# A scheduler that reckons with the arrival of TensorE's instructions: a linear-attention and hardswish kernel, its order set anew

## The chip, the cores and the metric

The kernel runs on one core of a Trainium2 chip. The metric is the device time of one execution in microseconds (us), the median of several runs. The profile is that of one execution.

Engines are named as in the profile: PE is TensorE (PEld its weight loads), DVE is VectorE, ACT is ScalarE, POOL is GpSimd, and SP is SyncE, which issues almost all transfers. SBUF tiles and PSUM banks are named as in the code.

## The reference

Two parts, one behind the other. The first is a linear attention with a decaying state, for 4 batches, 8 heads, 768 steps and a head size of 48:

```python
for t in range(S):
    cur = np.einsum('bhd,bhe->bhde', u[None] * kt, vt)
    y[:, :, t] = np.einsum('bhd,bhde->bhe', rt, state + cur)
    state = wt[:, :, :, None] * state + np.einsum('bhd,bhe->bhde', kt, vt)
```

The second takes its output as 3072 tokens of 384 and applies two matrices (384 to 2048 and back) with a hardswish between them:

```python
h = x @ w_in
g = h * np.clip(h + 3.0, 0.0, 6.0) / 6.0
return (g @ w_out).astype(np.float32)
```

## The kernel before

The sequence is cut into 24 chunks of 128 steps, and four chunks make one of six blocks of 512 tokens. For each chunk `i` the kernel has a set of small steps, whose names in the program's plan are used in this document:

- `feat{i}` and `tok{i}` load the chunk (SP, L394 and L406). `back{i}` and `fore{i}` are scans over the decays on DVE (L469, L478); `K{i}` (L489) and `R{i}` (L493) scale keys and queries by them; `own{i}` (L502) and, on PE, `dot{i}` (L516) give the step's own term; `diag0{i}` and `diag1{i}` (L534, ACT) put it on a diagonal, four instructions each.
- `score{i}` (L544, PE) multiplies K and R into two PSUM banks; `above{i}` (L551) takes the masked result from there.
- `turn{i}` (L560, PE) transposes K, `turned{i}` (L565, ACT) copies it out, `kv{i}` (L646, PE) multiplies it with the values, and `kvs{i}` (L654, ACT) copies the product out of its banks; `decay`, `mid`, `decb`, `state` carry the state on.
- `read{i}` (L624 and L633, PE) gives the chunk's output and `leave{i}` (L711, L713 or L729, ACT) copies it out as the second part's input. For chunks 0 and 1 the last pair of heads goes ahead: `first{i}` on PE, `third{i}` (L693, L695, ACT), and then `read{i}`, which here begins with L703.

The weights arrive as 64-bit words in sixteen portions of two slices (`fetch{j}`, L437, 768 KB each, into a ring of three tiles named `bits`). Each is made into float32 by one step on ACT, `low{j}` (L447, output `more`), and two on DVE, `whole{j}` (L451) and `full{j}` (L456).

The second part of block 0 is done directly: `up0.{f}.{c0}` (L762, PE), `ramp` (L752, ACT), `gate` (L773, DVE), `down0.{c}.{q}` (L781, PE). Blocks 1 to 5 use fast matrix products with fewer multiplications: `tx` (sums of inputs, DVE), `up{bk}.{d}.{r}` (L876, PE), `read`, `clip` and `gate` of these (L884 to L901, ACT and DVE), `sum` (L916, DVE), `down` (L931, PE) and `out` (L940 to L949).

None of this stands in the code in the order in which it runs. All steps are handed to a class `Plan`, each with its engine, a duration, the steps it comes after, the ring slots that it takes and what frees them, and a key (a due time). `order()` goes through them like a simulation: on each engine the step that can start at the earliest time is taken, and among those ready the one with the least key. Transfers are reckoned with one shared link (`link`, `RATE`, `LAND`). `SHIFT` is a table of single numbers, each added to one step's key. `emit()` then issues the instructions in that order. As every engine runs its own instructions in the order of issue, this fixes the order on every engine. Where `emit` finds PE idle by the plan's times, before the first `up`, it issues filler matmuls (`spin`, L1315, into a bank that nobody reads):

```python
k = int((self.start[n] - last + self.MORE) / self.SPIN) if n != self.until else 0
while k > 0:
    self.spin(min(k, 4))
    k -= 4
```

Of the kernel before, what the change touches and what calls it, by code (L numbers as in the profile page):

```python
# [24 lines left out]
BC = 4  # L25
# [5 lines left out]
TURN = 1.0  # L31
# [18 lines left out]
    "feat0": -208.0, "tok0": -511.0, "own0": 640.0, "feat1": -504.0, "feat2": -267.0, "tok2": 624.0, "own2": 100.0,  # L50
    "score2": -447.0, "decay2": -430.0, "read2": -592.0, "fore3": 878.0, "R3": 1602.0, "turn3": 238.0, "fore4":
    1394.0, "dot4": 93.0, "above4": -46.0, "turn4": 171.0, "dot5": 251.0, "diag05": 1476.0, "kv5": 701.0, "decay5":
    916.0, "back6": 349.0, "fore6": 289.0, "tok7": -372.0, "tok8": -269.0, "read8": 595.0, "leave8": 181.0, "tok9":
    -130.0, "mid9": 1100.0, "leave9": 780.0, "tok10": -62.0, "fore10": 1238.0, "kvs10": -128.0, "fore11": 364.0,
    "back12": -176.0, "kvs12": -271.0, "kvs13": -325.0, "leave13": 519.0, "feat14": -376.0, "feat15": -211.0,
    "back15": 735.0, "fore15": 867.0, "own15": 553.0, "diag015": 343.0, "turn15": -96.0, "fore16": -151.0, "sum16":
    -625.0, "turn16": 381.0, "kvs16": -750.0, "state16": 575.0, "fore17": 567.0, "back18": 607.0, "diag018": 281.0,
    "fore19": 793.0, "ownu19": 638.0, "diag019": 77.0, "back20": 445.0, "sum20": 541.0, "feat22": -92.0, "fetch1":
    71.0, "fetch2": -265.0, "fetch3": 477.0, "fetch5": 558.0, "whole5": 411.0, "full7": 831.0, "fetch8": 617.0,
    "fetch9": 453.0, "full9": 571.0, "fetch10": 474.0, "whole10": 464.0, "fetch11": 1041.0, "fetch12": 1125.0,  # L60
    "fetch13": 605.0, "fetch14": 909.0, "fetch15": 1157.0, "up0.4.0": 612.0, "up0.5.0": 782.0, "up0.6.0": 410.0,
    "gate0.6.0": 250.0, "up0.7.0": 510.0, "gate0.7.0": 82.0, "up0.12.0": 225.0, "up0.13.2": 490.0, "down0.0.1":
    436.0, "down0.2.0": 173.0, "tx1.4": 929.0, "up1.0.14": 105.0, "up1.0.8": 106.0, "up1.0.16": 112.0, "up1.1.14":
    190.0, "up1.1.0": 759.0, "up1.1.8": 421.0, "up1.1.17": -327.0, "up1.1.1": 185.0, "up1.1.9": 237.0, "up1.1.2":
    253.0, "down1.0.1.0": 1079.0, "down1.0.3.0": 113.0, "down1.0.7.0": 111.0, "sum1.1.4.0": -503.0, "sum1.1.1.1":
    -483.0, "sum1.1.3.1": 446.0, "sum1.1.4.1": -357.0, "down1.1.1.0": 819.0, "down1.1.5.0": 630.0, "down1.1.2.1":
    536.0, "down1.1.3.1": 901.0, "down1.1.7.0": -52.0, "down1.1.7.1": -163.0, "down1.1.4.1": -398.0, "up2.0.14":
    -59.0, "up2.0.6": 277.0, "up2.0.0": 389.0, "up2.0.8": -182.0, "up2.0.15": -137.0, "up2.0.12": -138.0,
    "up2.0.17": -172.0, "up2.0.1": -455.0, "up2.0.9": -77.0, "up2.0.13": -144.0, "up2.0.2": 229.0, "read2.0.a13":
    -521.0, "gate2.0.1": -124.0, "gate2.0.5": 68.0, "gate2.0.6": -53.0, "up2.1.14": -107.0, "up2.1.8": 236.4,  # L70
    "up2.1.11": 912.0, "up2.1.18": 331.0, "up2.1.9": 250.0, "read2.1.a7": -96.0, "down2.0.6.0": -9.0, "down2.0.6.1":
    -122.0, "down2.0.3.0": -22.0, "down2.0.3.1": -136.0, "down2.0.7.1": 101.0, "down2.1.1.0": -497.0, "down2.1.5.0":
    540.0, "down2.1.2.1": 524.0, "down2.1.7.0": -938.0, "down2.1.7.1": -482.0, "down2.1.4.1": 291.0, "tx3.1":
    -946.0, "tx3.6": -620.0, "tx3.7": -728.0, "tx3.9": -953.0, "tx3.10": -697.0, "up3.0.5": 367.0, "up3.0.12":
    392.0, "up3.0.17": 365.0, "up3.0.7": 341.0, "read3.0.a3": 599.0, "read3.0.a11": 519.0, "gate3.0.0": 423.0,
    "gate3.0.2": 673.0, "clip3.0.3": 753.0, "clip3.0.7": 825.0, "up3.1.6": 342.0, "up3.1.8": 398.0, "up3.1.12":
    730.0, "up3.1.11": 266.0, "up3.1.1": 376.0, "up3.1.18": 278.0, "up3.1.13": 395.0, "clip3.1.5": 693.0,
    "down3.0.6.0": -301.0, "down3.1.5.0": 184.0, "up4.0.14": -773.0, "up4.1.14": -82.0, "up4.1.12": -53.0,
    "up4.1.1": -129.0, "down4.0.1.0": 465.0, "down4.0.5.1": 668.0, "down4.1.1.0": -128.0, "down4.1.3.1": 311.0,
    "up5.0.12": 268.0, "up5.0.3": 180.0, "up5.0.9": 47.0, "up5.1.19": 256.0, "up5.1.6": 260.0, "up5.1.0": -418.0,  # L80
    "up5.1.8": 324.0, "up5.1.12": -67.0, "up5.1.1": 132.0, "up5.1.3": 260.0, "up5.1.9": 236.0, "read5.1.a9": 1037.0,
    "down5.0.1.0": 407.0, "down5.0.4.1": 534.0, "refetch0": -312.0, "refetch1": -670.0, "refetch2": -706.0,
    "refetch3": -338.0, "refetch4": -348.0, "refetch5": 538.0, "refetch8": -563.0, "refetch9": -330.0, "vet9.1":
    424.0, "refetch15": -227.0, "vet15.1": -951.0, "vet17.0": 413.0, "refetch18": -176.0
# [73 lines left out]
class Plan:  # L158
# [14 lines left out]

    def lag(self, a, n):

        engine = self.steps[a][0]
        if engine != self.steps[n][0]:
            return self.HOP[engine]
        kind = a.split(".")[0].rstrip("0123456789")
        alike = kind == n.split(".")[0].rstrip("0123456789")  # L180
        return self.CHAIN if engine == "DVE" and not (alike and kind in self.LONE) else None

    def __init__(self):
        self.steps = {}
        self.rings = {}
        self.taken = {}
# [4 lines left out]
    def add(self, name, engine, us, emit, after=(), key=0.0, hold=(), port=False, kb=0.0, lands=0.0,  # L191
            dmas=1):

        assert name not in self.steps, name
        self.steps[name] = (engine, us, emit, tuple(after), key + SHIFT.get(name, 0.0), tuple(hold), port, kb, lands, dmas)

# [6 lines left out]
    def order(self):  # L203
# [5 lines left out]
        lanes = []  # L209
        left = {n: sum(a not in end for a in x[3]) for n, x in steps.items()}  # L210
# [7 lines left out]
        while open_:  # L218
# [30 lines left out]
            free[engine] = end[n] = t + us  # L249
# [25 lines left out]
    def emit(self):  # L275

        last = self.COLD
        spinning = self.spin is not None
        for n in self.order():
            engine, us, emit = self.steps[n][:3]  # L280
            if engine == "PE" and spinning:
                k = int((self.start[n] - last + self.MORE) / self.SPIN) if n != self.until else 0
                while k > 0:
                    self.spin(min(k, 4))
                    k -= 4
                last = self.start[n] + us
                spinning = n != self.until
            emit()


def fast_path(tc, feat, tok, wflat, ub, ug, moe_w_in, moe_w_out, out, flag, n_chunks):
# [21 lines left out]
    with ExitStack() as ctx:  # L313
# [696 lines left out]
        def do(fn, *args):  # L1010
            return lambda: fn(*args)
# [27 lines left out]
        for i in range(NT):  # L1039
# [21 lines left out]
            if i < BY_PE:  # L1061
                plan.add(f"own{i}", "DVE", 0.56, do(own, i), [f"feat{i}"] + ["later"] * (i == 0) + [f"own{i - 1}"] * (i > 0), k + OWN,
                         [("rk", [f"dot{i}"])], port=True)
                plan.add(f"dot{i}", "PE", 0.82, do(own_dot, i), [f"own{i}"], k + OWN, [("ps", [f"sum{i}"])])
# [10 lines left out]
            if i <= BC:  # L1075
                plan.add(f"score{i}", "PE", 0.55, do(score, i), [f"K{i}", f"R{i}"] + [f"score{i - 1}"] * (i > 0), due,
                         [("bank", [f"above{i}"])] * 2)
            plan.add(f"above{i}", "DVE", 0.68, do(above, i), [scored(i), f"diag1{i}"], due + 0.5)
            plan.add(f"turn{i}", "PE", 0.39 if i <= BC + 1 else 0.44, do(turn_k, i), [f"K{i}"] + [f"turn{i - 1}"] * (i > 0), due + 0.01 if i <= BC + 1 else due - TURN, [("ps", [f"turned{i}"])])
            plan.add(f"turned{i}", "ACT", 0.42, do(turned_k, i), [f"turn{i}"] + [f"turned{i - 1}"] * (i > 0), due - 2 if i > BC + 1 else due + 0.5,  # L1080
                     [("kn", [written_by(i)])])
            if i in SOLO:
                plan.add(f"kv{i}", "PE", 0.5, do(write_alone, i), [f"turned{i}", f"tok{i}"], t - 0.2,
                         [("bank", [f"kvs{i}"])] * 2)
# [18 lines left out]
            if i < BY_SUM:  # L1103
                plan.add(f"first{i}", "PE", 0.65 if first else 0.75, do(read_last, i), [f"above{i}", f"decb{i}"], t + 0.01, y)
                plan.add(f"third{i}", "ACT", 0.54 if i != APART else 0.9, do(leave_last, i), [f"first{i}"], t + 0.01,
                         ([("x", all_up), ("S_", [f"read{j}" for j in range(BY_SUM)])] if i == 0 else []))
                plan.add(f"read{i}", "PE", 2.6 if first else 2.95, do(read_rest, i), [f"third{i}"], t + 0.01)
                plan.add(f"leave{i}", "ACT", 1.05, do(leave_rest, i), [f"read{i}"], t + 0.02)
            elif bk == 0:
                plan.add(f"read{i}", "PE", 1.5, do(read_both, i), [f"above{i}", f"decb{i}"], t + 0.01, y)  # L1110
                plan.add(f"leave{i}", "ACT", 1.5, do(leave, i), [f"read{i}"], t + 0.02)
            else:
                uses = [f"up{bk}.{d}.{r}" for d in range(2) for r in range(20) if X_PLACE[r][0] == "w"] + [f"tx{bk}.{x}" for x in range(len(X_SUMS))]
                space = [("x", uses)] * (c == 0)
                needs, us, hold = [begun(i), f"above{i}"], 0.52, []
                reads = [f"above{i + 1}"]
                if i + 2 < NT and i + 2 not in SOLO:
                    needs += [f"turned{i + 2}", f"tok{i + 2}"]
                    reads += [f"kvs{i + 2}"]
                    us += 0.42  # L1120
                if i + 1 < NT:
                    needs += [f"R{i + 1}", f"K{i + 1}", f"decb{i + 1}"]
                    hold = [("bank", reads)] * 2 + [("y", [f"leave{i + 1}"])]
                    us += 1.05
                if i == BC:
                    plan.add(f"begin{i}", "PE", 0.6, do(begin, i), [f"decb{i}", f"R{i}", f"read{i - 1}"], t - LEAD, y)
                plan.add(f"read{i}", "PE", us, do(read, i), needs, t + 0.01, hold)
# [24 lines left out]
        for x, (c0, c1) in enumerate(parts):  # L1152
            m = c1 - c0
            for f in range(NFC):
# [3 lines left out]
                         k, [("bank", [f"gate{n_}"])])  # L1158
# [4 lines left out]
        for c in classic:  # L1163
            for q in range(HF):
# [4 lines left out]
                         [("bank", [f"drain0.{c}"])] if q == 0 else ())  # L1169
# [44 lines left out]
        for bk in range(NB):  # L1214
# [7 lines left out]
            for d in range(2 * (bk > 0)):  # L1222
# [19 lines left out]
                for c, items in enumerate(CHAINS):  # L1242
                    for j_, x in enumerate(items):
                        if not isinstance(x, int):
# [4 lines left out]
                                 [("bank", [r + items[-1]])] if j_ == 0 else ())  # L1249
# [17 lines left out]
            for p in range(2 * (bk > 0)):  # L1267
# [12 lines left out]
                for n_, (k_, after, hold) in enumerate((  # L1280
                        (1, [], [("bank", [r + "c21"])]), (5, [], [("bank", [r + "c12"])]), (2, [r + "s1"], []),
                        (6, [r + "s1"], []), (3, [r + "v"], []), (7, [r + "u"], []), (4, [r + "c22"], []))):
                    for x in range(2):
                        before = gated(0, NFC) if k_ != 1 else gated(4 * x, 4 * x + 4)
                        if k_ in (5, 6, 7, 3):
# [3 lines left out]
                                 before + [d_ + f"{k_}.0"] * x + [d_ + f"{chain}.1"] * bool(chain) + after + [f"sout{t_}.{x}" for t_ in ({5: 1, 6: 2, 7: 3, 4: 4}.get(k_),) if t_], at + 2.6 * n_ + 1.3 * x + (2.6 if k_ == 4 else 0), hold if x == 0 else ())  # L1289
# [368 lines left out]
```

## Time and profile before

| | |
|---|---|
| Runs | 547.68, 545.11, 547.29 us; median 547.29 |
| Profiled execution | 547.55 us; span from first to last instruction 545.8 us |
| PE busy | 532.4 us (98%), 5408 matmuls |
| DVE, ACT, POOL busy | 425.3, 255.9, 113.7 us |
| First `up` (L762) starts | 34.56 us |
| Granted PE clock, mean | 0.992 |
| Data queue (q1) | 63.12 MB, 38.4% of the 16 transfer engines' span |
| Instruction queue of PE (q8) | 44 packets, 0.72 MB |

Times within the execution are counted from the span's start. A busy time is the union of an engine's instructions; a stretch in which PE is busy is not for that reason at full pace, since fillers count as busy and the granted clock may be below 1. "A <- B" in a list of waits means that A's engine stood until B's event, by the order of the semaphores' times; that the event named was the last one near by is no proof that it was waited for.

### The profile page before, as it was taken

How to read it: one execution, taken by the hardware profiler on the slowest of the kernel's cores; microseconds unless marked ns; L12 is line 12 of the kernel's file. 1: busy time of each engine (PE TensorE's matmuls, PEld its weight loads, DVE VectorE, ACT ScalarE, POOL GpSimd, SP SyncE). 2: the span in 40 equal slices, each digit the busy share in tenths (PEclk: the TensorE clock that was granted, in tenths of full speed). 3: DMA queues.
4: the chain of work that ended last, by engine and by line, in shares of the span. 5: the costliest groups of instructions: out<-in, count | busy, mean ns of one | idle time of the engine just before them, and what ended most of it. 6: DMA issues, size and time to landing. Idle time of an engine off the chain costs nothing.

```text
span 545.8 us, 13085 instructions
## 1 busy us (share of the span) xinstructions
PE 532.4 (98%) x5408; PEld 465.8 (85%) x5408; DVE 425.3 (78%) x701; ACT 255.9 (47%) x656; POOL 113.7 (21%) x111
## 2 busy tenths in 40 slices
PE   8979999999999999999999999999999999999996
PEld 5768787666788999988999988999888999988995
DVE  6969899997768989999876989998858843188450
ACT  3857655543255844365335554744254632353300
POOL 2000010765100554413042215253200300000000
PEclk9979999999999999999999999999999999999999
DMA  8996695443110168765034773056300000000001
GB/s 222 276 247 199 173 302 177 130 115 111 57 38 1 34 196 246 232 203 160 1 97 155 272 235 81 23 188 232 125 0 1 17 25 23 30 0 1 0 16 49
DMA packets 23267, 64.03 MB, mean 117 GB/s; under 512 B 3216, under 2 KB 10544, under 8 KB 23200
## 3 DMA queue, kind: packets, MB, share of 16 engines
q1 hardware_dynamic: 23072, 63.12, 38.4%
q8 instruction: 44, 0.72, 0.5%
q14 instruction: 23, 0.19, 0.1%
q10 hardware_dynamic: 128, 0.00, 0.0%
HBM read 57.31 MB, written 4.72 MB: 114 GB/s over the span
## 4 chain that ended last, share of the span: by engine, by line
PE 89%; DMA 6%; DVE 2%; ACT 1%; issue 1%; SPq 1%; DVEq 0%; ACTq 0%
PE bank L931 28%; PE bank L876 27%; PE bank L781 8%; PE bank L762 6%; PE bankS L931 5%; PE bankS L876 5%; DMA bits<-in_moe_w_in_dram 4%; PE bank L544 2%; PE bank L646 2%; PE y_ps L633 2%; PE y_ps L624 2%; DMA bits<-in_moe_w_out_dram 2%; PE ps L560 1%; PE ps L516 1%; ACT xT L729 0%
## 5 line engine op out<-in xcount | busy, mean ns | idle before, releaser
L897 ACT ACTIVATE clip<-g,three 128x512 f32<-128x512 f32 x80 | 56.8, 721 | 56.2 <-DVE g L893 45.2
L893 DVE TENSOR_TENSOR g<-bank,g 128x512 f32<-128x512 f32 x80 | 53.8, 684 | 16.2 <-PE bank L876 11.2
L901 DVE SCALAR_TENSOR_TENSOR g<-clip,g 128x512 f32<-128x512 f32 x80 | 57.2, 731 | 6.4 <-ACT clip L897 6.1
L489 POOL TENSOR_TENSOR K<-feat_in,E 112x512 f32<-112x512 f32 x17 | 24.7, 1453 | 161.1 <-PE bank L544 133.7
L931 PE MATMUL bank<-w_out,g 128*128 128x192 f32 x320 | 56.9, 328 | 0.0
L931 PEld LDWEIGHTS bank<-w_out,g 128*128 128x128 f32 x320 | 52.6, 190 | 1.1 <-issue 0.2
L534 ACT ACTIVATE A<-eyes,dg 128x64 f32<-128x64 f32 x192 | 49.0, 336 | 1.7 <-PE y_ps L633 1.3
L762 PE MATMUL bank<-xT,w_in 128*128 128x256 f32 x192 | 44.9, 386 | 0.0
L729 ACT COPY xT<-y_ps 48x256 f32<-48x256 f32 x88 | 32.2, 366 | 24.1 <-PE y_ps L624 21.7
L781 PE MATMUL bank<-w_out,g 128*128 128x384 f32 x128 | 42.8, 489 | 0.0
L762 PEld LDWEIGHTS bank<-xT,w_in 128*128 128x128 f32 x192 | 36.0, 193 | 5.0
L876 PE MATMUL bank<-xT,w_in 128*128 128x256 f32 x160 | 40.2, 381 | 0.0
L891 ACT COPY g<-bank 128x512 f32<-128x512 f32 x50 | 28.5, 586 | 21.1 <-PE bank L876 21.0
L781 PEld LDWEIGHTS bank<-w_out,g 128*128 128x128 f32 x128 | 24.0, 190 | 15.5
L947 ACT ACTIVATE o<-bank 128x192 f32<-128x192 f32 x30 | 9.9, 330 | 57.4 <-PE bank L931 57.2
L505 POOL TENSOR_TENSOR rk<-rk_in 128x384 f32<-128x384 f32 x15 | 16.3, 1089 | 94.9 <-PE ps L516 71.9
L876 PEld LDWEIGHTS bank<-xT,w_in 128*128 128x128 f32 x160 | 29.9, 190 | 4.7 <-ACT g L891 1.1
L478 DVE TENSOR_TENSOR_SCAN W<-feat_in,start 112x520 f32<-112x520 f32 x24 | 33.4, 1395 | 0.5 <-PE y_ps L624 0.5
L469 DVE TENSOR_TENSOR_SCAN E<-feat_in,back 112x520 f32<-112x520 f32 x24 | 30.4, 1268 | 3.3 <-DMA feat_in<-in_feat_dram 3.1
L876 PE MATMUL bank<-xT,bits 128*128 128x256 f32 x120 | 30.6, 381 | 0.0
L493 POOL TENSOR_TENSOR W<-feat_in,W 112x512 f32<-112x512 f32 x17 | 24.4, 1438 | 25.1 <-DVE W L478 25.1
L931 PE MATMUL bankS<-w_out,g 128*128 128x192 f32 x160 | 28.6, 329 | 0.0
(274 smaller groups left out, 1122.4 us busy)
## 6 DMA issues: line engine op xcount, KB each, us to landing
feat_in<-in_feat_dram SPq DMA_DIRECT2D x23, 675.9 KB, 5.8
bits<-in_moe_w_in_dram SPq DMA_DIRECT2D x8, 768.0 KB, 12.9
bits<-in_moe_w_out_dram SPq DMA_DIRECT2D x8, 768.0 KB, 5.5
feat_in<-in_moe_w_in_dram SPq DMA_DIRECT2D x8, 768.0 KB, 4.7
feat_in<-in_moe_w_out_dram SPq DMA_DIRECT2D x8, 768.0 KB, 5.6
rk_in<-in_tok_dram SPq DMA_DIRECT2D x15, 384.0 KB, 5.9
v_in<-in_tok_dram SPq DMA_DIRECT2D x24, 192.0 KB, 4.6
out_dram<-o SPq DMA_DIRECT2D x24, 192.0 KB, 2.1
```

Of the source, the lines that this page charges most:

```text
L469: nc.vector.tensor_tensor_scan(out=E_[:, ::-1], data0=d["w"][:, :0:-1], data1=back.rearrange("q p t -> q (p t)")[:, ::-1], initial=0.0, op ...
L478: nc.vector.tensor_tensor_scan(out=W_, data0=d["w"][:, :-1], data1=starts[i % 2].rearrange("q p t -> q (p t)"), initial=0.0, op0=ALU.mult, ...
L534: nc.scalar.activation(out=d["A"][:, h, :], in_=eyes, func=ACT.Copy, scale=d["dg"][:, h])
L729: nc.scalar.copy(out=blocks[bk]["xT"][g * GP:g * GP + D, :, at:at + HL], in_=st[i]["y_ps"][y_bank(i, a, g)][(g ^ a) * GP:(g ^ a) * GP + D, ...
L762: nc.tensor.matmul(h_ps[:, :(c1 - c0) * L], lhsT=w_in[:, f // 2, j, f % 2, :], rhs=b["xT"][:, j, c0 * L:c1 * L], start=(j == 0), stop=(j = ...
L781: nc.tensor.matmul(b["o", c][:, :DM], lhsT=g_of(0, f, c), rhs=w_out[:, f, :], start=(f == 0), stop=(f == NFC - 1))
L876: nc.tensor.matmul(b["p", d, c][:, z * HB:(z + 1) * HB], lhsT=weight(W_PLACE[r])[:, 2 * z + d, :], rhs=x_at(bk, X_PLACE[r]), start=fresh a ...
L891: nc.scalar.copy(out=out_, in_=src)
L893: nc.vector.tensor_tensor(out=out_, in0=src, in1=out_of(bk, d, other), op=ALU.add if sign > 0 else ALU.subtract)
L897: nc.scalar.activation(out=c, in_=out_of(bk, d, u), func=ACT.Relu, bias=three, scale=1.0)
L901: nc.vector.scalar_tensor_tensor(out=g, in0=blocks[bk]["r", d, u], scalar=6.0, in1=g, op0=ALU.min, op1=ALU.mult)
L931: nc.tensor.matmul(b["d", p, to][:, :h], lhsT=a, rhs=w(), start=(f == 0 and k in (1, 5)), stop=(f == HF - 1 and k in (2, 3, 4)), skip_grou ...
```

## The change

`Plan` now keeps, for each PE step, a number of instructions (`size`), and walks a counter through PE's instruction stream. Every 256 instructions (`PORTION`) a further portion is asked for when the counter passes a mark (`ASKED`), and the portion asked for before that one has to be there when it passes a second mark (`NEEDED`). A portion arrives a fixed time after it was asked for (`FETCH`), plus a share of what the data link still has to move at that moment (`BEHIND`, at most `MOST`). Where it is late, the PE step's planned end moves by as much; fillers are reckoned as instructions too. The durations, dependencies and rings of all steps are unchanged. The table `SHIFT` is replaced as a whole, so that the order of steps differs on every engine, from the first microseconds to the last block.

```diff
 SHIFT = {
-    "feat0": -208.0, "tok0": -511.0, "own0": 640.0, "feat1": -504.0, "feat2": -267.0, "tok2": 624.0, "own2": 100.0,
...
+    "feat0": -505.0, "tok0": -422.0, "own0": 1325.0, "decb0": 271.0, "feat1": -407.0, "tok1": -297.0, "feat2":
...
 }
@@ class Plan
+    PORTION, ASKED, NEEDED = 256, 168, 194
+    FETCH, BEHIND, MOST = 3.5, 1.2, 8.0
+    before = 8
+
+    def passed(self, f, t, us, size, link):
+
+        late, i0 = 0.0, f["at"]
+        while size > 0 and self.PORTION * f["n"] + self.ASKED < i0 + size:
+            asked, needed = self.PORTION * f["n"] + self.ASKED, self.PORTION * f["n"] + self.NEEDED
+            asked = max(t + late + us * max(0.0, asked - i0) / size, f["ready"])
+            needed = t + late + us * min(1.0, max(0.0, needed - i0) / size)
+            late += max(0.0, f["ready"] - needed)
+            f["ready"] = asked + self.FETCH + min(self.MOST, self.BEHIND * max(0.0, link - asked))
+            f["n"] += 1
+        f["at"] = i0 + max(size, 0)
+        return late
+
+    def fills(self, start, last):
+
+        return max(0, int((start - last + self.MORE) / self.SPIN))
@@ order()
             start[n] = t
-            free[engine] = end[n] = t + us
+            late = 0.0
+            if engine == "PE":
+                k = self.fills(t, last) if filling and n != self.until else 0
+                filling = filling and n != self.until
+                if k:
+                    late = self.passed(fetch, t - k * 0.213, k * 0.213, 4 * -(-k // 4), link)
+                late += self.passed(fetch, t + late, us, self.size[n], link)
+                last = t + us + late
+            free[engine] = end[n] = t + us + late
@@ emit()
-                k = int((self.start[n] - last + self.MORE) / self.SPIN) if n != self.until else 0
+                k = self.fills(self.start[n], last) if n != self.until else 0
...
-                last = self.start[n] + us
+                last = self.end[n]
@@ fast_path: every step on PE gets its size, as in
-                plan.add(f"dot{i}", "PE", 0.82, do(own_dot, i), [f"own{i}"], k + OWN, [("ps", [f"sum{i}"])])
+                plan.add(f"dot{i}", "PE", 0.82, do(own_dot, i), [f"own{i}"], k + OWN, [("ps", [f"sum{i}"])], size=16.7)
...
```

## The prediction

> **What bounds the kernel now.** I read the page first (TensorE, PE, is busy nearly the whole span), then the stretches, then who waits for whom, the chain, the transfers and ScalarE's timeline where PE stands still. All times come from one profiled execution: 547.55 us, of which 545.8 are the span and 1.7 lie around it; it stands 0.26 above the median of 547.29.
>
> ```profile
> span 545.8 us, 13085 instructions
> ...
> PE 532.4 (98%) x5408; PEld 465.8 (85%) x5408; DVE 425.3 (78%) x701; ACT 255.9 (47%) x656; POOL 113.7 (21%) x111
> ...
> q8 instruction: 44, 0.72, 0.5%
> ```
>
> The work of PE is the same after the change, so only the time in which it stands, spins or runs at half clock can move. The stretches (length, then busy time of each engine, granted clock, transfer share, GB/s) show where that is:
>
> ```profile
> 16.50:28.00 11.50, 11.02 (x197) 8.74 (x194) 11.11 (x20) 8.74 (x28) 0.00 (x0) 1.00 1.05 283
> 28.00:31.50 3.50, 0.05 (x4) 0.05 (x4) 1.03 (x3) 2.06 (x5) 0.00 (x0) 0.62 1.02 221
> 31.50:36.00 4.50, 4.50 (x45) 4.09 (x46) 3.30 (x8) 1.37 (x6) 0.00 (x0) 0.54 1.05 259
> 36.00:60.00 24.00, 23.73 (x326) 20.11 (x325) 19.47 (x36) 16.66 (x44) 0.00 (x0) 1.00 0.78 220
> 60.00:66.00 6.00, 5.38 (x116) 4.24 (x115) 5.79 (x13) 4.42 (x17) 0.00 (x0) 1.00 0.27 65
> 66.00:100.00 34.00, 33.88 (x272) 27.06 (x271) 32.36 (x57) 19.30 (x43) 6.14 (x5) 1.00 0.65 217
> 100.00:322.00 222.00, 222.00 (x2463) 192.31 (x2462) 191.20 (x295) 107.86 (x291) 71.31 (x62) 1.00 0.44 135
> 322.00:541.00 219.00, 217.47 (x1850) 200.80 (x1848) 149.04 (x252) 87.88 (x201) 33.28 (x30) 1.00 0.17 54
> ```
>
> One hole is long: 28 to 31.5, followed by a stretch at a clock of 0.54. PE's own waits put it down so:
>
> ```profile
> PE bank L544 <- ACT more L447: 3.6, 1, 3.6
> PE bankS L1315 <- POOL ident masks.py:199: 1.4, 1, 1.4
> PE bank L876 <- DVE T__4259 L828: 0.7, 1, 0.7
> ```
>
> L544 is `score2`. It reads K and R of chunk 2 and never `more`; K was done at 20.66, R (L493) at 25.38, and its banks were free by 28.8 at the latest. So the releaser named is only the last event near by. What does fit is in the transfers of 28 to 30 us, one packet of PE's instruction queue (it runs from 28.47 to 29.83):
>
> ```profile
> q8 instruction: 1, 0.02, 4.2%
> ```
>
> Between 20 and 28 us that queue moved nothing, and PE had run 346 matmuls and 346 weight loads when it stopped. I take it that PE stood for its next portion. ScalarE (ACT) in the same time:
>
> ```profile
> 22.85 1.08 ACT L447 ACTIVATE more<-bits 128x768 int16<-128x768 uint8 x1 [0.23 <-DMA bits<-in_moe_w_in_dram]
> 23.80 0.61 ACT L693 COPY xT<-bank 48x64 f32<-48x64 f32 x4
> ...
> 25.30 2.02 ACT L534 ACTIVATE A<-eyes,dg 128x64 f32<-128x64 f32 x8
> 27.85 0.32 ACT L711 COPY xT<-bank 128x192 f32<-128x192 f32 x1 [0.53 <-PE bank L633]
> 28.18 0.64 ACT L713 COPY xT<-bank 64x192 f32<-64x192 f32 x2
> ...
> 30.03 1.06 ACT L447 ACTIVATE more<-bits 128x768 int16<-128x768 uint8 x1 [0.98 <-DMA bits<-in_moe_w_in_dram]
> ```
>
> Here `leave1` (L711, L713), which the first `up` product needs, is done at 28.8, ahead of the `low` step at 30.03 that waits for the fourth portion of weights. Before the change nothing but PE's stop holds the first `up`, which starts at 34.56.
>
> **The stop's price.** Idle from 27.82 to 31.45: 3.63 us. After it the same groups run slow: L544 x32 1.13 for 0.70 elsewhere, L516 x8 2.05 for 1.04, L762 x6 2.12 for 1.47, together 2.1. In all 5.7 us, 1.0% of the time: the most that this part can bring.
>
> The page Runtime: NRT & Kernel Launch of the Trainium skill, section Instruction fetch mechanics, says that PE's program memory is refilled in blocks of 16 KiB (256 instructions), ahead of their use, and that crossing a block's edge is mostly hidden. The packet sizes agree (44 packets, 0.72 MB); the 3.63 us do not look hidden. By that rule there is nothing to remove, and this part would be worth 0 in place of at most 5.7.
>
> **What the new order puts there.** I followed the changed program's instructions as they stand on each engine. The fetch reckoning itself adds no instruction; fillers (L1315) go from 15 to 13, worth nothing by themselves since they only fill waits. On SP the first twelve transfers are the same, the twelfth being the fourth portion of weights (issued at 20.14, landed at 30.01); then two more weight portions go ahead of two `feat` loads. On ACT two things move. `leave0` now stands behind two `low` steps, and `third1` behind `leave0`. And `leave1` now stands behind the `low` of that fourth portion and four more diagonals.
>
> 1. `third1` to `read1`. The third portion's `low` ends at 23.93 (row above); `leave0` 0.96 and `third1` 0.61 follow: 25.4. PE has `kv1`, `read0`, `first1`, `dot2` and one filler until about 23.0 (it issues `turn2` and `kv2` later now), so it stands some 2.4 us. `read1` then takes 2.5 (L703 1.45, L624 0.54, L633 0.55): 27.9. `dot3` and `score2` (1.04 and 0.70) bring it to 29.6.
> 2. The first `up`. Landing 30.01, `low` 1.06, four diagonals 1.0 (half of 2.02), `leave1` 0.32 and 0.64, 0.15 to PE: 33.2. PE stands again, 3.6 us. The instruction portion's packet, some 1.6 us before PE goes on at 31.45, now falls under this wait: the 692nd PE instruction is at the end of `score2`. If the portion of weights lands earlier, since no `feat` load runs beside it, the least is 26.66 (the transfer before it) plus 786 KB at the 390 GB/s that weights alone reached at 17 to 20 us, 28.7, and the first `up` 31.9. I take 33.2, by the row of the same transfer.
> 3. Work not yet done. `turn2` and `kv2` come later on PE: 0.44 and 0.61, 1.05 us. So the first `up` at 33.2 for 34.56 is a gain of 1.36 - 1.05 = 0.3 (1.6 at best).
> 4. Clock. Before, it dropped 1.0 us into the stop, for 6.8 us, 1.1 us of them after 34.56 (0.55 lost). Two holes of 2.4 and 3.6 us will do so at least once: I take 2.9 us after 33.2, 1.45 lost, so 0.9 worse; between 0.55 better (clock back by then) and 1.2 worse.
>
> So the stop is replaced by ACT's queue, not removed: 0.6 us slower up to 36 us, between 2.1 faster and 1.5 slower.
>
> **From 36 to 66 us.** Before, PE stands 0.27 and 0.62 here; the longest, 0.53 before an L516, is behind L654, behind an L447 that waited 2.30 for a portion of `w_out` landed at 57.59. In the new order `kvs3`, then `leave2`, stand right behind the `low` of SP's twenty-first transfer, and `score3` on PE needs the banks that `kvs3` frees. Need: 33.2 plus ten `up` (1.30 each), two `turn`, two `kv`, one `dot` (1.0), `read2` (1.4) and the lost clock: 52.1. Offer: transfers twelve to twenty-one are 6.5 MB; after 26.66 they take 22.9 us at 283 GB/s or 27 at 240 (rows of 16.5 and of 28 to 36), so 49.6 to 53.7, plus `low` 1.06 and `kvs3` 0.55: 51.2 to 55.3. PE waits 0 to 3.2 us. I take 1.1, near the middle, less the 0.5 that goes: 0.6 slower.
>
> **From 66 us on.** Idle time is 0.12, 0 and 1.53, so at most 1.65 to gain; the orders of the blocks are new throughout, and they can lose as much. No row prices a single move; I take 0, plus or minus 1.6. The 5 us after the last matmul stay.
>
> Sum: 547.55 + 0.6 + 0.6 - 0.26 = 548.5.
>
> **The rivals.**
> - The stop goes and little follows. For: weights were moved at 390 GB/s where no `feat` load ran beside. Against: `leave1` behind a `low`. First `up` at 31.9 with the clock back (2.1), no wait at `score3` (0.5), half of the late idle time (0.8): 3.4 less, 543.9. The bound, with all 5.7 kept, is 541.6.
> - ACT blocked, slower. Price, if the twenty-first transfer lands at 53.7: PE stands 3.2 at `score3`, and the clock falls again (2.1 as at 31.5), less 0.5, plus 0.6 from the start: 5.4 more, 552.7. It decides from a landing after about 52.5. For: ACT is strictly in order, and seven more `low` steps stand among `kvs` and `leave` steps there. Against: only 0.5 us came through before.
> - The change does not do what it says: instructions are late at the portion before (packet at 17.77). PE would stand 1 to 2 us near 20, inside the wait for `third1` anyway: 548.5 again, counted with the forecast.
>
> **How the numbers follow.** No change within measurement is 0.5% (2.7 us), about what this kernel can tell. Forecast 0.48, first rival 0.2, second 0.32. Some of the first rival's cases stay under 2.7 us and some of the forecast's upper end goes over: faster 0.17, same 0.5, slower 0.33. The range reaches 5 us both ways, to below the faster case and past the slower one, with about one in ten outside at each end; the likeliest case alone is 546 to 551.
>
> **What would show it.** Right: in the new profile PE's idle time before L584 or the first L802 of the new numbering, near 29 to 33 us, ended by ACT `xT` (leave1), and another near 23 to 25 ended by ACT `xT` (third1); the first L802 at 32 to 33.5; clock below 1 in 28 to 36. Steps 1 and 2 are wrong if PE runs through from 20 to 36. The 36 to 66 part is wrong if no wait on ACT `kvs` shows there. The whole is wrong if PE's idle time after 66 us changes by over 2 us.

## The result, and the profile after

| | before | changed |
|---|---|---|
| Median of 20 executions | 546.44 us (545.11 to 549.10) | 548.17 us (545.83 to 552.37) |
| Profiled execution, span | 547.55, 545.8 us | 546.18, 544.5 us |
| A second profiled execution of the changed kernel | | 547.81, 546.1 us |
| First `up` starts | 34.35 (34.56 if counted from the end of the matmul before it) | 29.45; in the second 30.59 |

The ratio of the changed kernel to the one before is 1.0033, interval 1.0017 to 1.0050: 0.3% slower, inside the bound of 0.5%. The profiled execution is one of the quickest of its kernel: its granted clock was 0.996, and of the twenty executions the five at 0.996 or above took 545.8 to 547.2 us, the fifteen at 0.993 or below 547.5 to 552.4. So two profiles are read here: this one, and the second (run `a_again` below) for what most executions do.

From the page of the changed kernel:

```profile
span 544.5 us, 13050 instructions
...
PE 530.7 (97%) x5404; PEld 462.7 (85%) x5404; DVE 421.7 (77%) x701; ACT 256.1 (47%) x656; POOL 112.8 (21%) x111
...
q8 instruction: 44, 0.72, 0.6%
```

The same stretches as before the change (length, busy time of PE, PEld, DVE, ACT, POOL, granted clock, transfer share, GB/s):

```profile
16.50:28.00 11.50, 9.44 (x161) 7.52 (x161) 11.25 (x19) 7.11 (x22) 0.00 (x0) 1.00 1.03 300
28.00:31.50 3.50, 2.73 (x42) 2.36 (x42) 3.40 (x7) 2.62 (x9) 0.00 (x0) 1.00 1.11 297
31.50:36.00 4.50, 4.15 (x19) 3.34 (x18) 3.50 (x8) 4.00 (x12) 0.00 (x0) 1.00 0.98 226
36.00:60.00 24.00, 23.75 (x326) 19.92 (x325) 23.80 (x49) 19.83 (x55) 0.00 (x0) 1.00 0.88 291
60.00:66.00 6.00, 6.00 (x59) 4.79 (x58) 5.99 (x12) 2.66 (x5) 0.00 (x0) 1.00 0.86 236
...
322.00:541.00 219.00, 214.46 (x1837) 198.05 (x1835) 149.44 (x249) 86.49 (x199) 30.95 (x30) 1.00 0.18 57
```

The hole of 3.5 us is gone, and 16.5 to 28 us, once nearly full, now lacks 2.1 us of PE. In the last stretch PE ends at 538.38, so 2.6 of the 4.5 us that are missing lie after the last matmul; the other 1.9 are waits. PE's own waits name them:

```profile
PE bank L743 <- ACT xT L733: 0.9, 1, 0.9
PE ps L556 <- DVE rk L542: 0.8, 1, 0.8
PE bank L802 <- ACT xT L753: 0.8, 1, 0.8
PE bank L971 <- DVE S__3772 L956: 0.6, 1, 0.6
PE bank L916 <- DVE g L933: 0.6, 1, 0.6
PE bank L916 <- ACT g L931: 0.4, 1, 0.4
```

The first three lie at 22.5, 26.1 and 28.7 us (`third1`, `own3` on DVE, `leave1`); the last three at 325 to 343 us are new, for before the change PE waits for nothing between 300 and 350. ACT's timeline at the start:

```profile
20.95 1.09 ACT L487 ACTIVATE more<-bits 128x768 int16<-128x768 uint8 x1 [1.34 <-DMA bits<-in_moe_w_in_dram]
...
22.86 0.64 ACT L733 COPY xT<-bank 48x64 f32<-48x64 f32 x4
...
26.57 1.07 ACT L487 ACTIVATE more<-bits 128x768 int16<-128x768 uint8 x1 [1.78 <-DMA bits<-in_moe_w_in_dram]
...
28.45 0.30 ACT L751 COPY xT<-bank 128x192 f32<-128x192 f32 x1
28.76 0.64 ACT L753 COPY xT<-bank 64x192 f32<-64x192 f32 x2
```

The queue is as forecast (`leave0` and `third1` behind two `low` steps, `leave1` behind the next and four diagonals), but that next `low` starts at 26.57 and not at 30.01: the fourth portion of weights landed at 26.49, 3.5 us earlier than before.

**Where PE falls behind.** A view made from the traces: at a given time, that time less the work PE has done, each matmul counted with the median pace of its kind at full clock in the profile before (510.3 us in all, for every kernel here). What a stretch adds to it is idle time, fillers, half clock and slow pace together. The columns are to be compared with one another: sorting the matmuls into kinds in another way moves a whole row up or down by up to 2 us, and the differences in it by 0.2 to 0.4.

| | before | changed | changed, second | `b_split1_read2` | `old_to_280` |
|---|---|---|---|---|---|
| 0 to 36 us | 22.76 | 18.75 | 20.99 | 17.02 | 22.44 |
| 36 to 66 | 3.07 | 1.40 | 1.40 | 2.26 | 2.53 |
| 66 to 280 | 1.11 | 2.74 | 2.39 | 1.23 | 1.10 |
| 280 to 350 | 0.10 | 3.48 | 3.60 | 0.32 | 3.38 |
| 350 to 530 | 3.08 | 1.58 | 1.58 | 3.30 | 1.58 |
| After the last matmul | 5.28 | 6.08 | 5.70 | 5.27 | 6.45 |

The second execution against the one before: -1.8, -1.7, +1.3, +3.5, -1.5 and +0.4, which makes the 0.2 to 0.3 by which the spans differ. The change gains 3.5 us up to 66 us in this execution (5.7 in the quickest) and gives 3.3 back behind it, with the tail 3.7.

This accounts for two executions, not for the medians, which are 1.7 us apart. The execution of before that is read here took 1.1 us more than its median, and the second of the changed kernel 0.4 less than its own; what those 1.5 us are, no trace here tells.

In the row 280 to 350 PE stands 1.96 us after the change, at six places, and not at all before it. From start to start the matmuls ahead of these six waits fall 2.9 us behind their pace: the profile still counts the matmul ahead of a wait as busy (0.38 us where the pace is 0.22), so a wait costs PE more than the idle time shown (at 324.68 us 0.59 for 0.42). These waits are most of the 3.4 us of that row.

### The profile page after: what moved, and what is told of

Same layout as the page of the kernel before. It is cut to its first block, busy times and chain, and to the rows that moved or that the text cites. A ratio compares the mean times of both kernels' runs of the same rounds, so it can differ in the third digit from the quotient of the medians.

```text
span 544.5 us, 13050 instructions
## 1 busy us (share of the span) xinstructions
PE 530.7 (97%) x5404; PEld 462.7 (85%) x5404; DVE 421.7 (77%) x701; ACT 256.1 (47%) x656; POOL 112.8 (21%) x111
## 4 chain that ended last, share of the span: by engine, by line
PE 85%; DVE 9%; DMA 2%; ACT 1%; issue 1%; POOL 0%; POOLq 0%; DVEq 0%; ACTq 0%
PE bank L971 27%; PE bank L916 24%; PE bank L821 8%; PE bank L802 7%; PE bankS L971 4%; PE bankS L916 4%; DVE g L933 3%; PE bank L686 2%; PE bank L584 2%; PE y_ps L673 2%; PE y_ps L664 2%; DMA bits<-in_moe_w_in_dram 2%; DVE g L941 1%; PE ps L600 1%; PE bankS L1357 1%; PE ps L556 1%
## 5 line engine op out<-in xcount | busy, mean ns | idle before, releaser
L529 POOL TENSOR_TENSOR K<-feat_in,E 112x512 f32<-112x512 f32 x17 | 21.3, 1252 | 156.1 <-PE bank L584 154.9
L821 PE MATMUL bank<-w_out,g 128*128 128x384 f32 x128 | 44.1, 491 | 0.0
L509 DVE TENSOR_TENSOR_SCAN E<-feat_in,back 112x520 f32<-112x520 f32 x24 | 32.1, 1336 | 2.9 <-DMA feat_in<-in_feat_dram 2.8
L533 POOL TENSOR_TENSOR W<-feat_in,W 112x512 f32<-112x512 f32 x17 | 26.2, 1543 | 30.6 <-DVE W L518 23.2
L613 POOL TENSOR_TENSOR S<-S,w_min 112x192 f32<-112x192 f32 x15 | 14.9, 996 | 81.5 <-DVE S L621 81.5
L545 POOL TENSOR_TENSOR rk<-rk_in 128x384 f32<-128x384 f32 x15 | 18.2, 1213 | 52.1 <-DMA rk_in<-in_tok_dram 27.8
```

What stands on the lines that cost most here:

```text
L509: nc.vector.tensor_tensor_scan(out=E_[:, ::-1], data0=d["w"][:, :0:-1], data1=back.rearrange("q p t -> q (p t)")[:, ::-1], initial=0.0, op ...
L821: nc.tensor.matmul(b["o", c][:, :DM], lhsT=g_of(0, f, c), rhs=w_out[:, f, :], start=(f == 0), stop=(f == NFC - 1))
```

## Experiments

The theory: before the change PE stood for its instructions at 28 us; the new order avoids that; part of the gain goes to new waits and the half clock near 30 us, and the rest to its later order. The rivals are with each run.

**`a_again`: the changed kernel once more.** No edit.

> The changed kernel once more, unchanged, for a second profiled execution and more times. Theory 1 (the clock): the executions of this order differ by what the granted clock loses in and after the holes at 22 to 30 us; times lie between 545.8 and 552.4 us, a mean clock of 0.996 to 0.998 goes with 546 to 547 and one of 0.988 with 551, about 0.55 us for each 0.001. A profile at 0.993 or below then shows a stretch of half clock between 22 and 40 us and PE's holes there at over 2 us in one stretch of 3.4 us. Theory 2 (the transfers): the spread comes from the landing of the portions of weights and would show as longer waits on ACT or DVE at an unchanged clock.

Median 548.07 (547.11 to 551.43), ratio 1.0032, interval 1.0005 to 1.0059. The profile, at a mean clock of 0.991, has holes of 0.77 and 0.78 us before L743 and L556, at 23.3 and 26.8. Its stretches (last columns: clock, transfer share, GB/s):

```profile
28.00:31.50 3.50, 3.50 (x42) 3.09 (x42) 3.40 (x6) 2.48 (x8) 0.00 (x0) 0.50 1.04 328
31.50:36.00 4.50, 4.50 (x16) 3.69 (x16) 3.50 (x9) 3.52 (x11) 0.00 (x0) 0.71 1.02 226
```

PE is busy all the time there, at half clock: the trace's clock record has it from 27.28 to 34.11. That is theory 1, with less idle time than it asked for: the two holes make 1.55 us together, not over 2. The two profiles differ by 2.24 us at 36 us, and by at most 0.4 in any later row of the table. The clock is not all of the spread: of the twenty executions above, the seven with a mean clock of 0.993 took from 547.89 to 550.55 us.

**`b_split2` and `b_split1`: the old order with its fillers in smaller pieces.** The work of the fillers stays; what grows is the number of instructions ahead of everything that follows (by 28 and by 96).

```diff
                 while k > 0:
-                    self.spin(min(k, 4))
-                    k -= 4
+                    self.spin(min(k, 2))      # b_split1: 1
+                    k -= 2                    # b_split1: 1
```

> The kernel before, its fillers issued in pieces of two blocks for four: the same filler work in 22 issues for 15, so 28 more instructions ahead of score2, and every later instruction 28 further back in the stream. Nothing else moves. Theory 1 (PE stood for its instructions, and their packet stood behind SP's twelfth transfer, issued at 20.14): the portion is asked for some 0.4 us earlier, ahead of that transfer; its packet goes at about 24.5 for 28.47, the 3.63 us before score2 go, and the first up starts at 30 to 31; with the clock 5.7 us are to be had, 541.6 us, if no later portion takes the place of this one (then 543 to 548, with the stop at 33 to 38 us). If the packet stays at 28.47, the stop begins 14 matmuls earlier, inside read1. Theory 2 (PE waited for the low step on ACT or for its transfer, as the profile names it): the stop stays before score2 at 3.6 us and the time at 546.4.

> The kernel before, its fillers issued one block at a time: 39 issues for 15, 96 more instructions ahead of score2. Theory 1 (PE's instructions): the portion that came at 28.47 is asked for at about 18 us and comes by 24, no stop before score2; the next is asked for at about 24 to 25, behind transfers thirteen to fifteen (to 37 us), and PE may stand for it at 33 to 38, at a place 48 matmuls earlier than without the change of fillers. 542 to 548 us. Theory 2 (ACT or the transfer of weights): stop of 3.6 before score2 as before, 546.4.

`b_split2`: median 547.55 against 546.48, ratio 1.0028 (1.0011 to 1.0046). `b_split1`: 544.27 (542.04 to 547.88), ratio 0.9976 (0.9949 to 1.0002); its profiled execution took 542.04, 5.5 less than that of before, with the clock whole. PE's timeline of `b_split2`, two lines:

```profile
29.74 0.57 PE L633 MATMUL bank<-A,v_in 64*48 64x64 f32 x11 [2.76 <-issue]
...
38.37 1.99 PE L762 MATMUL bank<-xT,w_in 128*128 128x256 f32 x8 [0.52 <-issue]
```

and of `b_split1`:

```profile
31.97 0.66 PE L633 MATMUL y_ps<-A,v_in 64*48 64x64 f32 x31 [0.35 <-issue]
```

The stop of `b_split2` is no longer before L544 but in the middle of L633, where no semaphore stands ("issue"): PE starts its 693rd recorded instruction (matmuls and weight loads) after it, exactly as before the change. The other two lines stand at the 947th, 254 further. All four waits, that of before included, end 1.46 to 1.62 us after the end of a packet of 16 KB on PE's instruction queue (and so do the stops of `old_to_100` and `old_to_280` below, again at the 693rd):

| | PE at its 424th instruction | SP issues transfer 12 | packet | PE stands at its 693rd |
|---|---|---|---|---|
| before | 20.14 | 20.14 | 28.47 | 27.82 to 31.45 |
| `b_split2` | 18.90 | 19.20 | 26.99 | 26.98 to 29.74 |
| `b_split1` | 17.86 | 19.81 | 20.98 | no |
| changed | 19.00 | 19.80 | 24.37 | no; 0.77 for `leave1` |

The 424th (256 + 168) is about where the change's own reckoning, whose count begins at 8, has the portion asked for. Passing it 0.8 us or more ahead of SP's twelfth transfer goes with a packet about 4 us or more earlier; 0.3 us was not enough. So ACT's `low`, which the profile named, is out, and the first half of theory 1 holds: PE stood for its instructions. That the packet stood behind just that transfer fits the table, but no run moved the transfer alone, so it is not shown. The forecast for `b_split2` (packet at 24.5) missed: the stop moved 14 matmuls forward, shrank by 0.87 us only, and the next portion made another.

**`a_split1`: a control, the changed kernel with its fillers one block at a time.** The same edit in its `emit`.

> A control: the changed kernel with its fillers one block at a time, as in the fast kernel, nothing else. Theory 1 (finer fillers help only where a portion of instructions would come late): the changed kernel stands nowhere for instructions, so nothing is gained; its holes at 22 to 30 us stay, median 548.1 plus or minus 0.6. Theory 2 (finer fillers help by themselves, by the clock or by a smoother start): the gain of the fast kernel, 2 to 3 us, shows here too, 545 to 546.

Median 549.08, ratio 1.0040 (1.0017 to 1.0064): no gain, as in theory 1, though 0.4 us above its range. Its profile lost the clock from 26.87 us on and has holes of 0.5 and 1.1 us before L743 and L556. So finer fillers are no gain in the changed kernel; in the old order the quick executions came where they moved an instruction portion.

**`a_act`: two steps of ACT moved in the changed kernel.** Here and below the planner's order is taken, and then single steps are put ahead of others by hand.

```diff
+    MOVES = [('third1', 'leave0'), ('leave1', 'low1')]   # each put ahead of the other
```

> The changed kernel with two steps of ACT moved ahead, by hand, nothing else: third1 ahead of leave0, and leave1 ahead of the low of the fourth portion of weights (and of the diagonals behind it). Theory 1 (ACT's order holds PE at 22.5 and at 28.7): the wait before read1 falls from 0.94 to about 0.2 and that before the first up from 0.77 to 0; the hole before dot3 (behind own3 on DVE) grows to 1.5, since that step does not move, so the profile gains at most 0.8; the clock falls in fewer executions, and the median goes from 548.2 to 546 to 547.5. Theory 2 (the low step is what is needed: it feeds the up steps with weights): the first up starts earlier but PE waits 1 us more for w_in at 33 to 36, and the median stays within 0.5 of 548.2.

Median 548.75, ratio 1.0038 (1.0010 to 1.0065): theory 1's number missed, and the wait for `w_in` of theory 2 does not show. Both waits on ACT went (0.2 us is left of the first), but the one before `dot3`, behind `own3` on DVE, grew from 0.80 to 1.77 us, and the clock record shows half clock from 27.76 to 34.58. `own3` ended at 27.67 us, for 26.79 in the first profile of the changed kernel, with DVE busy almost without a break before it. This reads as three holes from one lateness, of which taking two away leaves the third; no run moved `own3`, so that is an argument and not shown.

**`a_fill`: a filler in each hole.**

```diff
+            if n in ("read1", "dot3", "up0.0.0"):
+                self.spin(4)
```

> The changed kernel with one filler of four blocks (0.85 us) ahead of each of read1, dot3 and the first up, where its profiles show PE standing 0.8 to 0.9, 0.8 and up to 0.8 us. Nothing else moves. Theory 1 (the changed kernel's typical execution loses the clock in these holes): PE is never idle there, the mean clock stays at 0.996 or above in most executions, and the median falls from 548.1 to 546.3 to 546.9. Theory 2 (what counts is the wait, not the clock; or a spinning PE counts as idle): median 548.1 plus or minus 0.5, with clocks of 0.988 to 0.993 as before.

Median 547.46 (545.99 to 551.36), ratio 1.0019 (0.9996 to 1.0042): between the theories in time. In clock it is theory 1: eight of ten executions at 0.996 or above, five of twenty without the fillers. The profile is one of the two others (550.62): there PE stood 1.64 us for `third1` in spite of the filler, and the clock fell. Keeping the clock in most executions so brought some 0.6 us of the median, less whatever the fillers themselves cost (the eight at 0.996 or above have a median of 547.2, the five without fillers 546.7); it is a part, and not the whole loss.

**`old_to_100` and `old_to_280`: the old order at first, then the new.**

```diff
+        lead, rest, at = (old, new, at_old)
+        out = [n for n in lead if at[n] < 100]               # 280
+        return out + [n for n in rest if n not in set(out)]
```

> The order of the kernel before for all steps planned before 100 us (its stop at 28 us included), the order of the changed kernel for the rest. Theory 1 (the new order is worse from 100 us on): the two profiles show the changed kernel giving back 2.6 us between 100 and 540 and 0.6 in the tail, so this kernel takes 3 us more than the kernel before, 549.5. Theory 2 (the new order's later part is as good, and the change gives its gain back by the clock near 30 us alone): 546.4 plus or minus 0.7.

> The order of the kernel before for all steps planned before 280 us, the order of the changed kernel for the rest. Theory 1: the part of the loss that lies behind 280 us, 1.9 in PE's progress (the waits for g at 325 and 331, for S at 342) and 0.6 in the tail: 548.5 to 549. Theory 2 (nothing is lost there by the order itself): 546.4 plus or minus 0.7.

Medians 550.20 (of four executions) and 548.34 against 546.78, ratios 1.0068 (1.0045 to 1.0091) and 1.0023 (1.0007 to 1.0038). Theory 1 both times, 0.7 us above its number and 0.2 below. PE's waits in `old_to_100` are the old stop and the new order's late ones, side by side:

```profile
PE bank L649 <- ACT more L552: 2.8, 1, 2.8
...
PE bank L1036 <- DVE S__3774 L1021: 0.6, 1, 0.6
PE bank L981 <- DVE g L998: 0.6, 1, 0.6
PE bank L981 <- ACT g L996: 0.4, 1, 0.4
```

They come at the same steps whether the first 280 us are old or new (the table's row 280 to 350: 3.38 to 3.60 for 0.10), so they belong to the order there and not to what went before.

**`b_split1_read2`: the old order, finer fillers, and one step of PE moved.**

```diff
+    MOVES = [('read2', 'up0.8.0')]
```

> The kernel before with its fillers issued one block at a time (as in the run that took 542.0 to 547.9 us, median 544.27), and read2 on PE moved behind up0.1.0; SP's load of the fourth chunk's values then stands behind one more portion of weights. In the run with the fillers alone PE still stood 0.35 us at its 947th instruction, 254 behind the 693rd, right after the packet of 29.32. Theory 1 (the next portion of instructions is nearly late as well): with 24 slow matmuls of an up step ahead of the 64 quick ones of read2, PE comes to that place 1.3 us later and does not stand there; fewer executions lose the clock, and the median falls to 542.5 to 543.8. Theory 2 (the slow executions have another cause): median 544.3 plus or minus 0.4, and as many at 547.

Median 543.08 (541.55 to 547.00), ratio 0.9946 (0.9915 to 0.9976): the quickest kernel here by its median, 5.1 us below the changed one (medians of separate sessions). Its interval overlaps that of `b_split1`, so the part of `read2` alone is not clear of noise. Between 20 and 66 us no wait of over 0.14 us is left in its profile. Theory 1, though three of ten executions still took 546.7 to 547.0 at 0.991 to 0.996.

**`b_best2` and `best_to_350`: two attempts to better it.** The first moves `back23` on DVE behind the sums `tx4`; the second takes the new order from 350 us on.

```diff
+    MOVES = [('read2', 'up0.8.0'), ('back23', 'vet5.0')]   # b_best2
+        out = [n for n in lead if at[n] < 350]               # best_to_350, with the finer fillers and read2 moved
```

> The kernel before with its fillers one block at a time and read2 behind up0.1.0 (median 543.08 in its own run), and in addition one step of DVE moved: back23, a scan of 1.23 us, from ahead of the sums tx4.0 to tx4.10 to behind them. Theory 1 (PE's wait of 1.11 us at 382 us for the sum T of block 4 is the queue on DVE): the wait goes, and the median falls by 0.6 to 1.1, to 542.0 to 542.5. Theory 2 (the sums are slow there because POOL works at the same time, 0.96 and 1.21 us for 0.41, or chunk 23 comes too late for block 5): 543.1 plus or minus 0.4, with a new wait on DVE or ACT after 440 us.

> The best kernel so far (the order before, fillers one block at a time, read2 behind up0.1.0; median 543.08) up to the steps planned at 350 us, and the order of the changed kernel from there. Theory 1 (the new order is better by itself behind 350 us, where its profiles lose 1.6 us of PE's time for 3.1 before the change): 1.5 us are gained, 0.4 to 1.2 of them go to its longer tail, median 541.9 to 542.9. Theory 2 (the gain behind 350 us is work put off from before 350, which the old order has done by then): nothing is gained, the joint costs, 543.1 to 545.

Medians 543.30 (ratio 0.9952, 0.9928 to 0.9976) and 543.41 (0.9959, 0.9943 to 0.9974): nothing gained, theory 2's number both times (without the wait after 440 us that it named). In `b_best2` the wait of 1.11 us became one of 1.23, 4 us later, behind ACT. The new order's 1.5 us behind 350 did not come along (the stretch to 530 costs 3.8 there): they were the other half of what it had lost before 350. Such a joint of two orders is thus not free of cost, which bears on `old_to_100` and `old_to_280` too; there the rows behind the joint at 280 are those of the changed kernel (3.38 and 1.58).

## Why the prediction was right, and where it was not

The time lay 0.3 us from the forecast of 548.5, "no change within measurement" was the likeliest case and came. That the sum was right is luck, by cancellation: the start came out better and the late part worse than its terms, and no term of the sum came out near its number. Its base, the median of three executions, was 0.9 us above that of twenty; against this base it forecast 1.2 us more, and 1.7 were measured.

- **The reading of the stop** was right: instructions and not `low`, and 5.7 us about its size. `b_split1_read2` loses 17.02 us in the first 36 for 22.76 before: 5.74 less. The rule cited there, that a block's edge is mostly hidden (the Trainium skill, page Runtime: NRT & Kernel Launch, section Instruction fetch mechanics), did not hold at this edge before the change: with a transfer share of 1.02 to 1.05 PE stood 3.63 us. In the changed kernel, at a share of 1.03 to 1.11, it stood nowhere for instructions.
- **Step 1**, the wait for `third1`: right in place and cause, 0.94 and 0.77 us for 2.4, since the third `low` ended at 22.04 and not 23.93. It missed `own3` on DVE (0.80, 0.78) altogether.
- **Step 2**, the first `up` at 33.2, 31.9 at best: wrong, 29.45 and 30.59. Its term was the landing of the fourth portion of weights, 30.01 by the row of the same transfer, 28.7 at the least; it landed at 26.49. Of these 3.5 us 1.9 came from the transfer before it, which landed at 24.73 for 26.66, and 1.6 from the distance between the two landings, 1.76 us for 3.35. The first part is partly an accident of the execution read: with the same first 100 us of order, `old_to_100` has 25.07 and `old_to_280` 26.20 for 26.66. The second follows the order. In the new one SP issues no load of `feat` between 19.80 and 24.50, and in the runs of that order the distance is 1.75 to 2.11 us where the trace tells; in all runs with such a load 0.4 us behind, as in the row taken, it is 2.82 to 3.83. The prediction's least case had the distance (786 KB at 390 GB/s, 2.0 us) and took the earlier landing from the row of before.
- **Step 4**, the clock: 1.45 us after the first `up`. In the second profile half clock runs 3.5 us past it, 1.76 lost; in the quickest executions nothing. By these steps the start was 0.6 slower; it was 4.0 and 1.8 quicker. (The slower bound given there, 1.5, does not come out of its terms, which make 0.9: 1.2 of clock less the gain of 0.3.)
- **36 to 66 us**: forecast 0.6 slower by a wait of `score3` on `kvs3`; it was 1.7 quicker. No such wait shows. In the second profile SP's twenty-second transfer, behind the twenty-first on the same queues, landed at 46.05, and the forecast for the twenty-first was 49.6 to 53.7: the same term again, transfers taken too slow.
- **From 66 us on**: taken as 0, within 1.6. It was 3.3 to 3.5 slower, and the tail 0.4 to 0.8 more. The bound came from the idle time of before, which limits a gain and not a loss.
- **The rivals**: the start went the way of the first ("the stop goes and little follows"), the late part undid it. ACT was not blocked in 36 to 66, and at the portion before (packet at 16.27 us in the first profile) PE did not stand.
- The sign that was to show steps 1 and 2 (waits ended by `third1` and `leave1`) came, some us early; the sign against the whole, PE's idle time behind 66 us off by over 2, depends on where one stops counting: up to the last matmul it is 2.7 for 1.2 in both profiles, up to the end of the span 8.8 and 8.4 for 6.5, which is over 2 in the first and just under in the second. The sign was too blunt, as a wait costs PE more than its idle time.

Open: why the stretch 66 to 280 costs 1.3 to 1.6 us more, of which the traces show one wait of 0.24 and 0.73 in `down0` of block 0 (128 matmuls in 42.53 us from start to start, for 41.80); what lies between the medians and the two executions read; and what the executions did that have no profile.

## What to carry to other kernels

A stop that a profile puts on a semaphore can be a late portion of instructions: look for a packet on the engine's instruction queue about 1.5 us before it ends, and move the count of instructions by harmless ones to see whether the stop keeps its number. Where the order is planned anew as a whole, a gain in one place can be paid for by whatever the search gave up elsewhere: cut the old order and the new together at a few times and time the halves, before crediting the idea (the joint itself can cost, as at 350 us here). Here a small edit of the old order (finer fillers, one step moved) took 3.7 us off the median in its session and lies 5 below the new order.

## What the runs showed that was not expected

- Half clock lasts 6.83 us, twice 3.41, in every record near 30 us (before, `a_again`, `a_act`, `a_fill`, `a_split1`, `b_split2` and the old_to runs). It starts 20.48 us (`a_` runs) or 23.90 (the others) after full clock first began, which is 6 and 7 times 3.41, and that first time lies anywhere from 4.5 to 7.3 us in the executions profiled. Holes of 0.94, 0.80 and 0.77 kept the clock in one execution of the changed kernel, holes of 0.77 and 0.78 lost it in another. So the same order can keep or lose the clock, depending on where its holes fall in these steps of 3.41 us; how much idle time in one step is enough, these records do not settle (0.94 us in the first profile of the changed kernel kept it, 0.76 in `a_split1` lost it).
- DVE's sums of two tiles wait for POOL. In `b_best2`, DVE and then POOL:

```profile
380.87 0.42 DVE L844 TENSOR_TENSOR T__4280<-xT 128x256 f32<-128x256 f32 x1
381.20 1.22 DVE L842 TENSOR_TENSOR T__4280<-T__4280,xT 128x256 f32<-128x256 f32 x1
382.34 1.22 DVE L840 SCALAR_TENSOR_TENSOR T__4280<-xT 128x256 f32<-128x256 f32 x1
```

```profile
380.88 1.26 POOL L521 TENSOR_TENSOR rk<-rk_in 128x384 f32<-128x384 f32 x1 [1.38 <-DMA rk_in<-in_tok_dram]
382.22 1.06 POOL L525 TENSOR_TENSOR rk<-rk,u_bc 128x384 f32<-128x384 f32 x1
```

Such a sum takes 0.41 alone; these two end 0.28 us after POOL's instructions (which end at 382.14 and 383.28). The Trainium skill, page SBUF — State Buffer, section "SBUF: two separate sides", has the two engines share one pair of ports, which a DVE instruction with two inputs in SBUF or a GpSimd instruction locks for its whole length; these rows agree.
- The tail after the last matmul is 5.27 to 5.48 us in the old order (6.03 in `b_best2`), 5.55 to 6.36 in the new, and 6.45 to 6.97 where the two are joined. In the first profile SP stands 3.26 us between its last branch and its next event, for 2.54 before the change, with three 8 KB packets of the other instruction queue (q14) beginning almost at once (540.28 to 540.42), where before the first came 1.6 us ahead of the other two. That alone is not the cause: in `b_best2` the packets are spaced as before the change, and SP stands 3.30 us. The cause stays open.
